# Query transfers on a second queue, idle transposes in the lead-in, a second PSUM bank up to slot 31, and a last tile stored in two halves

## Chip, core and metric

One core of one Trainium2 chip. The metric is device time in microseconds (us) of one execution; a kernel's time is the median of its executions. All runs told here gave the right result and were in the fast state. The program occupies one core. *Clock* means the share of its full clock that TensorE was granted, 1.00 or 0.50 in these traces; a mean below 1 tells how much of the time it was at half. A *window* at half clock is a stretch in which it was granted 0.50.

## The reference, cut to what matters

```python
# q, k, v: (8 batches, 8 heads, 576 rows, 64)   x = attention output as (4608, 512)
scores = scale * q @ k^T
scores = where(scores >= rowmax - tau, scores, -1e9)     # threshold mask
attn   = exp(scores - rowmax); attn /= attn.sum() + 1e-9
x      = (attn @ v) rearranged to (4608, 512)
h      = x @ w_in                                        # 512 -> 2048
g      = h * clip(h + 3, 0, 6) / 6
out    = g @ w_out                                       # 2048 -> 512
```

## The kernel before

Attention runs in 144 *slots*: 16 quads of heads (four heads of one batch) with nine slots each. A slot is 128 query rows of two heads. In each slot TensorE makes the scores, VectorE their row maximum, GpSimd the bias, ScalarE mask and exp, GpSimd the normalised weights, TensorE the value product. From slot 23 on the first product of the MLP of finished batches and its gate (`mm1`, from 80.69 us), from slot 31 on its second product too (`mm2`, from 111.61 us), are mixed into the slots; what is left of it runs after slot 143 without attention.

The parts that the change touches (cuts marked `...`):

```python
N1 = 22        # up to this slot VectorE copies keys out of PSUM, then ScalarE
N2 = 28        # up to this slot small products take two banks in turn
...
def main(dst, src, h, order):                     # one head of q or k, all on SyncE's queue
    nc.sync.dma_start(out=dst[:, :, h, :], in_=src[b, 4 * g + h, 0:512, :].rearrange(order, t=4))
...
def warm_up(count):                               # idle transposes: of a constant, the result isn't used
    warm = ps_h.tile([P, 2, 512], F32, tag="h", name="warm")
    for _ in range(count):
        nc.tensor.transpose(warm[:, 0, 0:P], identf[:], identf[:])
warm_up(14)
...
def bank(name):                                   # a bank of PSUM for a small product or transpose
    nonlocal turn
    turn += 1
    if now < N2 and turn % 2:
        return ps_o.tile([P, 512], F32, tag="o", name=name)
    return ps_m.tile([P, 512], F32, tag="m", name=name)

def copy_out(out, in_):                           # keys out of PSUM
    if 0 <= now < N1:
        nc.vector.tensor_copy(out=out, in_=in_)
    else:
        nc.scalar.copy(out=out, in_=in_)
...
evict = transpose_k(0); warm_up(4); evict_q = transpose_q(0)      # lead-in, shortened
evict(); evict_q()
transpose_rest(0)()          # remaining 64 rows of keys AND queries, one bank, VectorE then ScalarE
...
queue[0].tiles = scores(0, 0)
for n, sl in enumerate(queue):                    # the slots
    now = n
    ...                                           # exp of slot n-1, maxima of slot n
    if slot != 8 and todo1:
        h = mm1(item); r = mm1_relu(h, on_act=(slot in (0, 1, 3, 5))); mm1_gate(item, h, r)
    ...                                           # masks, transposes, value products
    if n + 1 < len(queue):
        queue[n + 1].tiles = scores(queue[n + 1].quad, queue[n + 1].slot)
    if n < 8:
        warm_up(6)
    ...
count = [0, 0]
def rest1(item, then):                            # MLP after the last slot
    h = mm1(item, pool=ps_s if count[0] % 3 else None)            # None: bank h
    count[0] += 1
    mm1_gate(item, h, mm1_relu(h, on_act=True))
```

The program gives each engine its own list of work in this order.

## Time and profile before

| quantity | value | where from |
|---|---|---|
| time, median of the first 3 runs | 561.12 us (561.0 to 562.59) | unprofiled runs |
| the execution that was profiled | 564.1 us, span 562.3 us, clock 0.989 | its own record |
| TensorE busy | 535.0 us, 95% | page |
| half clock in that execution | 10.9 to 17.8 and 106.5 to 109.9 us, and after the last product | clock records, windows of 0.5 us |

### The profile page before, as it was taken

To read this page: it belongs to the slowest core of one execution; us is meant where nothing else is said; L and a number is where in the kernel's file an instruction comes from. 1 tells how busy PE (TensorE), PEld (TensorE's weight loads), DVE (VectorE), ACT (ScalarE), POOL (GpSimd) and SP (SyncE) were. 2 spreads that over 40 slices of the span, in tenths; PEclk is the share of its full clock that TensorE was granted. 3 is DMA by queue.
4 is the path that set the end of the run, shared out by engine and by line. 5 is a ranking of instruction groups with operands and counts; after the bars stand their busy time and mean duration, and the time that the engine had idled before them with its cause. 6 is when DMAs were issued, how large, how long until landed. Compare 5 with 4: busy or idle time off the path is not lost.

```text
span 562.3 us, 11634 instructions
## 1 busy us (share of the span) xinstructions
PE 535.0 (95%) x3856; PEld 309.3 (55%) x3856; DVE 424.4 (75%) x1040; ACT 470.3 (84%) x999; POOL 305.2 (54%) x646
## 2 busy tenths in 40 slices
PE   7998798899999999999999999999999999999997
PEld 5665455455545565555555565655555565654663
DVE  3588787687878788787878798887978798883440
ACT  4799899798988999989898999899898999983540
POOL 1678878854556555655456555755556555561000
PEclk8899999899999999999999999999999999999999
DMA  5879999997689876978589867987699865453102
GB/s 110 135 110 166 162 160 184 207 148 144 112 159 153 151 153 127 208 139 155 114 150 170 159 137 146 174 160 146 127 137 175 167 124 117 101 109 86 38 20 75
DMA packets 286204, 77.52 MB, mean 138 GB/s; under 512 B 269248, under 2 KB 281536, under 8 KB 286144
## 3 DMA queue, kind: packets, MB, share of 16 engines
q1 hardware_dynamic: 268736, 67.86, 64.8%
q0 software_dynamic: 17408, 8.92, 13.7%
q8 instruction: 30, 0.49, 0.4%
q14 instruction: 30, 0.25, 0.2%
HBM read 36.70 MB, written 9.44 MB: 82 GB/s over the span
## 4 chain that ended last, share of the span: by engine, by line
PE 58%; DVE 11%; ACT 9%; issue 4%; POOL 1%; DMA 1%; SPq 1%; DVEq 0%; POOLq 0%
PE h L353 18%; PE o L382 17%; PE s L256 16%; DVE s L277 5%; ACT s L285 4%; PE av L323 3%; ACT s L290 3%; DVE g L370 2%; DVE r L364 2%; ACT r L362 2%; PE s L262 1%; PE tp L213 1%; PE ar L323 1%; DVE osb L390 1%; POOL pn L298 1%
## 5 line engine op out<-in xcount | busy, mean ns | idle before, releaser
L298 POOL TENSOR_SCALAR pn<-s,rinv 128x576 bf16<-128x576 f32 x288 | 211.6, 745 | 133.5 <-issue 58.5
L277 DVE TENSOR_SCALAR_CACHE_REDUCE s<-s 128x576 f32<-128x576 f32 x288 | 205.9, 752 | 44.9 <-PE s L256 35.2
L285 ACT ACTIVATE s<-s,bias 128x576 f32<-128x576 f32 x288 | 207.1, 766 | 36.8 <-POOL bias L280 35.7
L290 ACT ACTIVATE s<-s 128x576 f32<-128x576 f32 x288 | 192.7, 671 | 0.3
L256 PE MATMUL s<-kT,qT 64*128 64x288 f32 x1024 | 172.7, 435 | 5.4 <-DVE s L277 3.2
L353 PE MATMUL h<-xT,w_in_sb 128*128 128x320 bf16 (+1 forms) x1024 | 145.0, 287 | 5.5 <-DVE g L370 4.6
L382 PE MATMUL o<-w_out_sb,g 128*128 128x512 bf16 x576 | 140.9, 379 | 3.6 <-DVE osb L390 3.0
L353 PEld LDWEIGHTS <-w_in_sb 128*128 128x128 bf16 x1024 | 92.0, 97 | 68.4 <-issue 31.1
L256 PEld LDWEIGHTS s<-kT,qT 64*128 64x128 f32 x1024 | 94.8, 188 | 62.7 <-DVE s L277 24.9
L370 DVE SCALAR_TENSOR_TENSOR g<-r,h 128x512 bf16<-128x512 f32 (+1 forms) x128 | 96.4, 754 | 41.2 <-ACT r L362 39.3
L280 POOL TENSOR_SCALAR bias<-m 128x1 f32<-128x1 f32 x288 | 54.4, 189 | 69.0 <-DVE s L277 48.2
L382 PEld LDWEIGHTS <-g 128*128 128x128 bf16 x576 | 55.6, 98 | 58.2 <-issue 9.8
L362 ACT ACTIVATE r<-h,three 128x640 f32<-128x640 f32 (+1 forms) x74 | 54.4, 737 | 21.1 <-PE h L353 20.4
L290 ACT ACTIVATION_READ_ACCUMULATOR s<-s 128x1 f32 x288 | 54.2, 188 | 0.0
L364 DVE TENSOR_SCALAR r<-h 128x512 f32<-128x512 f32 (+1 forms) x54 | 40.5, 751 | 0.0
L390 DVE TENSOR_SCALAR osb<-o 128x512 f32<-128x512 f32 x31 | 21.0, 676 | 22.2 <-PE o L382 22.2
L323 PE MATMUL av<-pT,vm 128*64 128x512 bf16 x256 | 34.6, 392 | 2.0 <-ACT kT L203 2.0
L323 PEld LDWEIGHTS <-vm 128*64 128x64 bf16 x512 | 18.1, 111 | 25.2 <-issue 18.3
L293 DVE RECIPROCAL rinv<-rsum 128x2 f32<-128x2 f32 x144 | 23.0, 160 | 10.2 <-ACT s L290 9.5
L335 DVE CAST xT<-av 128x512 bf16<-128x512 f32 x32 | 21.8, 681 | 5.6 <-PE av L326 5.3
L277 DVE DVE_READ_ACCUMULATOR s<-s 128x1 f32 x288 | 23.9, 83 | 0.0
L388 ACT ACTIVATE osb<-o 128x512 f32<-128x512 f32 x5 | 3.0, 597 | 23.9 <-PE o L382 23.9
(42 smaller groups left out, 255.9 us busy)
## 6 DMA issues: line engine op xcount, KB each, us to landing
km<-in_k_dram SPq DMA_DIRECT2D x64, 128.0 KB, 3.0
out_dram<-osb SPq DMA_DIRECT2D x32, 256.0 KB, 2.4
nq<-in_q_dram SPq DMA_DIRECT2D x96, 72.0 KB, 2.7
vm<-in_v_dram POOLq DMA_DIRECT2D x16, 256.0 KB, 5.4
nq<-in_q_dram SPq DMA_DIRECT2D x16, 128.0 KB, 3.9
w_in_sb<-in_moe_w_in_dram POOLq DMA_DIRECT2D x16, 128.0 KB, 4.1
w_out_sb<-in_moe_w_out_dram POOLq DMA_DIRECT2D x16, 128.0 KB, 4.5
pT<-pn SPq DMA_TRANSPOSE x119, 3.4
```

The source lines that it names most:

```text
L256: nc.tensor.matmul(tiles[a][:, hf, 0:HALF], qT_of(pair)[a * 64:(a + 1) * 64, t * P:(t + 1) * P], keys(pair, a, hf), start=True, stop=True)
L277: nc.vector.tensor_scalar(out=sl.s[:, i, :].rearrange("p (a b) -> p a b", a=2), in0=ps[:, :, 0:HALF], scalar1=1.0, scalar2=None, op0=Alu.m ...
L280: nc.gpsimd.tensor_scalar(out=sl.bias[:, i:i + 1], in0=sl.m[:, i:i + 1], scalar1=-scale, scalar2=tau, op0=Alu.mult, op1=Alu.add)
L285: nc.scalar.activation(out=s, in_=s, func=Act.Prelu, bias=sl.bias[:, i:i + 1], scale=scale, alpha=REJECT)
L290: nc.scalar.activation(out=s, in_=s, func=Act.Exp, accum_out=sl.rsum[:, i:i + 1])
L298: nc.gpsimd.tensor_scalar(out=pn[:, i, :], in0=sl.s[:, i, :], scalar1=sl.rinv[:, i:i + 1], scalar2=1.0, op0=Alu.mult, op1=Alu.mult)
L323: nc.tensor.matmul(ps[a * 64:(a + 1) * 64, :], vm[:, 2 * hp + a, c * D:(c + 1) * D], pT[:, 5 * a + c, cols], start=(c == 0), stop=False)
L353: nc.tensor.matmul(hps[:, n, 0:w], w_in_sb[:, ki, (ni + n) * P:(ni + n + 1) * P], xT[b][:, ki, c0:c0 + w], start=(ki == 0), stop=(ki == KI ...
L362: nc.scalar.activation(out=r, in_=hps, func=Act.Relu, bias=three[:])
L364: nc.vector.tensor_scalar(out=r, in0=hps, scalar1=3.0, scalar2=0.0, op0=Alu.add, op1=Alu.max)
L370: nc.vector.scalar_tensor_tensor(out=gbuf[:, ni:ni + 2, c0:c0 + w], in0=r, scalar=6.0, in1=hps, op0=Alu.min, op1=Alu.mult)
L382: nc.tensor.matmul(o_ps[0], gbuf[:, ni, mt * P:(mt + 1) * P], w_out_sb[:, ni, :], start=(ni == 0), stop=(ni == NI - 1))
```

## The change

Four intents: the first scores shall not wait for query rows that are needed only in slot 8, and TensorE's clock shall stay up through the lead-in; the value product of slot 30 shall not wait for a PSUM bank; the first of the last output tiles shall find a free buffer; the last tile's eviction and store shall be split over two engines.

```diff
-    N2 = 28
+    N2 = 31
...
         def load_q(n):
...
+                    main(..., by=nc.scalar if quad == n == 0 else nc.sync)
...
-    def transpose_rest(quad):
+    def transpose_rest(quad, of_k=True, of_q=True):     # each half can be left out
...
-    transpose_rest(0)()
+    transpose_rest(0, of_q=False)()
+    warm_up(6)
...
+        elif n == 1:
+            evict = transpose_rest(0, of_k=False)
...
+        if n == 0:
+            warm_up(8)
         if n + 1 < len(queue):
             queue[n + 1].tiles = scores(...)
...
-    count = [0, 0]
+    count = [1, 0]
+    def last_out():
+        nc.scalar.activation(out=osb[:, 0:c], in_=o_ps[0][:, 0:c], func=Act.Copy, scale=1.0 / 6.0)
+        nc.scalar.dma_start(out=out[r0:r0 + P, 0:c], in_=osb[:, 0:c])
+        nc.vector.tensor_scalar_mul(out=osb[:, c:2 * c], in0=o_ps[0][:, c:2 * c], scalar1=1.0 / 6.0)
+        nc.sync.dma_start(out=out[r0:r0 + P, c:2 * c], in_=osb[:, c:2 * c])
...
-                late.extend(mm2_out(...))
+                if (bb, mt) == (B // 2 - 1, 8):
+                    last_out()
+                else:
+                    late.extend(mm2_out(...))
```

More of the change, by code (lines that the diff above doesn't have):

```diff
@@ L85, in load_quad, with main @@
         nq, km, kr = nat[quad]
-        def main(dst, src, h, order):
-            nc.sync.dma_start(out=dst[:, :, h, :], in_=src[b, 4 * g + h, 0:512, :].rearrange(order, t=4))
+        def main(dst, src, h, order, by=nc.sync):
+            by.dma_start(out=dst[:, :, h, :], in_=src[b, 4 * g + h, 0:512, :].rearrange(order, t=4))
         def blocks_q(n, a, j):
@@ L97, in load_q @@
                 for a in range(2):
-                    main(nq[:, 0:1024].rearrange("p (t h d) -> p t h d", h=4, t=4), q, 2 * n + a, "(t p) d -> p t d")
+                    main(nq[:, 0:1024].rearrange("p (t h d) -> p t h d", h=4, t=4), q, 2 * n + a, "(t p) d -> p t d",
+                         by=nc.scalar if quad == n == 0 else nc.sync)
             else:
@@ L226, in transpose_k @@
         return lambda: copy_out(kT_of(pair)[:, 64:576], ps[:])
-    def transpose_rest(quad):
+    def transpose_rest(quad, of_k=True, of_q=True):
         ps = bank("tr")
         nq, _, kr = nat[quad]
-        nc.tensor.transpose(ps[:, 0:P], kr[:], identf[:])
-        if by_pe(2 * quad):
+        of_q = of_q and by_pe(2 * quad)
+        if of_k:
+            nc.tensor.transpose(ps[:, 0:P], kr[:], identf[:])
+        if of_q:
             nc.tensor.transpose(ps[:, P:2 * P], nq[:, 1024:1152], identf[:])
@@ L237, in evict @@
             both = ps[:].rearrange("p (w n t) -> p w n t", n=2, t=64)
-            if by_pe(2 * quad):
+            if of_q:
                 nc.vector.tensor_copy(out=qT[:, :, 512:S], in_=both[:, 1])
-            copy_out(kT[0:64, :, S:S + 64], both[0:64, 0])
-            copy_out(kT[64:P, :, 0:64], both[64:P, 0])
+            if of_k:
+                copy_out(kT[0:64, :, S:S + 64], both[0:64, 0])
+                copy_out(kT[64:P, :, 0:64], both[64:P, 0])
         return evict
@@ L525 @@
     last = NQUAD - 1
-    count = [0, 0]
+    count = [1, 0]
+    def last_out():
+        osb = o_pool.tile([P, d_model], F32, tag="osb", name="osb")
+        r0, c = B * S - 64 - P, d_model // 2
+        nc.scalar.activation(out=osb[:, 0:c], in_=o_ps[0][:, 0:c], func=Act.Copy, scale=1.0 / 6.0)
+        nc.scalar.dma_start(out=out[r0:r0 + P, 0:c], in_=osb[:, 0:c])
+        nc.vector.tensor_scalar_mul(out=osb[:, c:2 * c], in0=o_ps[0][:, c:2 * c], scalar1=1.0 / 6.0)
+        nc.sync.dma_start(out=out[r0:r0 + P, c:2 * c], in_=osb[:, c:2 * c])
     def rest1(item, then):
@@ L539, in rest2 @@
                 flush()
-                late.extend(mm2_out(bb, mt, on_act=(count[1] % 2 == 0)))
+                if (bb, mt) == (B // 2 - 1, 8):
+                    last_out()
+                else:
+                    late.extend(mm2_out(bb, mt, on_act=(count[1] % 2 == 0)))
                 count[1] += 1
```

## The prediction

> **What bounds the kernel now.** I read the page first, then the stretches of time in which the granted clock fell, then the timeline of the first 20 us and of the change from attention alone to attention plus MLP (around 105 us), and last the chain of waits at the end.
>
> ```profile
> PE 535.0 (95%) x3856; PEld 309.3 (55%) x3856; DVE 424.4 (75%) x1040; ACT 470.3 (84%) x999; POOL 305.2 (54%) x646
> PE   7998798899999999999999999999999999999997
> ...
> L323 PE MATMUL av<-pT,vm 128*64 128x512 bf16 x256 | 34.6, 392 | 2.0 <-ACT kT L203 2.0
> ```
>
> TensorE is the bound for most of the span: from 113 to 504 us it is busy for 384.93 of 391 us. The parts with gaps are the head, the stretch to 113 us and a few waits at the end; the change works only on these. The last line shows one wait of TensorE for a ScalarE copy of keys, 2.0 us in the whole run.
>
> The windows of 1 us (columns: TensorE, weight loads, VectorE, ScalarE, GpSimd busy, granted clock, DMA):
>
> ```profile
> 9.00:10.00 1.00, 1.00 (x6) 0.51 (x6) 0.36 (x1) 0.00 (x0) 0.00 (x0) 1.00 1.03 232
> 11.00:12.00 1.00, 1.00 (x5) 0.72 (x5) 0.08 (x2) 1.00 (x2) 0.77 (x2) 0.50 0.44 97
> 16.00:17.00 1.00, 1.00 (x6) 0.28 (x2) 0.00 (x0) 0.64 (x2) 0.80 (x2) 0.50 0.00 0
> 18.00:19.00 1.00, 1.00 (x11) 0.81 (x10) 0.95 (x4) 0.78 (x2) 0.41 (x3) 1.00 0.86 106
> ```
>
> From 11 to 17.6 us TensorE runs at half its clock. The timeline of the same stretch:
>
> ```profile
> 7.59 0.30 PE L233 MATMUL tr<-identf,nq 128*128 128x128 f32 x1 [0.81 <-DMA nq<-in_q_dram]
> 8.25 0.53 ACT L203 COPY kT<-tr 64x128 f32<-64x128 f32 x2 [2.16 <-DVE qT L239]
> 8.83 1.23 PE L256 MATMUL s<-kT,qT 64*128 64x288 f32 x6 [0.27 <-ACT kT L203]
> 9.64 0.76 DVE L277 TENSOR_SCALAR_CACHE_REDUCE s<-s 128x576 f32<-128x576 f32 x1 [1.42 <-PE s L256]
> 10.46 2.96 PE L256 MATMUL s<-kT,qT 64*128 64x288 f32 x8 [0.39 <-DVE s L277]
> 17.14 0.76 DVE L277 TENSOR_SCALAR_CACHE_REDUCE s<-s 128x576 f32<-128x576 f32 x1 [2.84 <-PE s L256]
> 18.23 1.45 ACT L285 ACTIVATE s<-s,bias 128x576 f32<-128x576 f32 x2 [1.59 <-POOL bias L280]
> 106.35 0.56 ACT L203 COPY kT<-tp 128x512 f32<-128x512 f32 x1
> 106.96 1.92 PE L323 MATMUL av<-pT,vm 128*64 128x512 bf16 x8 [2.03 <-ACT kT L203]
> ```
>
> The first scores wait for the remainder of the queries (the last 64 rows), which no score needs before slot 8: transfer, transpose, VectorE copy, then the ScalarE copy of the remainder of the keys, which the first scores do need. Then the scores of slot 1 take 2.96 us where eight such matmuls take 1.24 us at full clock (at 18.61 us), so VectorE and ScalarE stand idle before slot 2. The end, from the chain of waits:
>
> ```profile
> 540.07 0.70 DVE g L370
> 540.77 0.04 issue
> 540.81 17.44 PE o L382 x80
> 558.25 0.02 issue
> 558.27 0.60 ACT osb L388
> ```
>
> The last five output tiles start only when a gate has emptied a PSUM buffer (TensorE idle 0.62 us), then 80 matmuls without a gap, one eviction of 0.60 us and the last store.
>
> [...] the first 14, alone on TensorE, take 3.06 us (0.21 us apart), and after them six take 0.88 us (0.12 apart)[...]. So I count on idle transposes. [...] The trace shows issues of 0.5 to 0.7 us each, one behind another, on SyncE. [...] the ScalarE copy at 8.25 us waited for the VectorE copy out of the same bank.
>
> **The change part by part.**
>
> Queries on ScalarE's queue, remainder of the queries later. TensorE's lead-in from the first key transpose (4.83 us) to the end of the transpose of the remaining keys (6.47 + 0.30 = 6.77) has almost no gap, so earlier queries by themselves gain nothing; what gains is that the 0.81 us wait and the transpose after it leave the path. The new path: ScalarE copies the keys' remainder from about 6.8 to 7.35 us while six idle transposes run to about 7.45; the scores of slot 0 begin there, and VectorE's maximum follows 1.36 us later (as at 119.89 to 121.25), at 8.8 instead of 9.64. Gain 0.8 us.
>
> Idle transposes (six before the first scores, eight behind them). Eight at 0.12 us fill about 8.6 to 9.65, just until VectorE has emptied the first score tile (8.8 + 0.76), so they delay nothing, and if the clock holds, slot 1's scores take 1.24 us from 9.65 and their maximum starts at 11.0 (now 12.51). Slot by slot on ScalarE: mask of slot 0 at 10.72 - 0.83 = 9.9; a slot's mask and exp take about 2.8 (10.72 to 13.50), so mask 1 at 12.7, mask 2 at 15.4 if its scores are there: scores 2 from about 11.9, maximum 13.25, bias ready 14.3, yes. Now mask 2 is at 18.23. Gain in all 2.8 to 2.9 us, the 0.8 included. From slot 3 on the same instructions follow in the same distances, and ScalarE is nearly full to 78 us (61.28 of 74 us, waits under 0.6 us each), so the gain is carried on.
>
> Two banks up to slot 31 (two names in turn until 28 before). In slot 30 the value product needs the single bank that the key transposes of slot 29 hold until the ScalarE copy at 106.35 ends; TensorE then stands 2.03 us and the clock falls (0.50 at 107 to 109 us), so the product takes 2.3 us instead of 1.43. With the second bank it runs from 104.9 to 106.35. But the next scores need that same copy of keys (106.9), and the next MLP product needs the gate which ends at 109.55, behind ScalarE's work and GpSimd's bias (108.58, GpSimd full with DMA issues and normalising from 97.5 us). So that product starts at 109.55 instead of 110.72, and the following scores at 112.0 instead of 113.0. Of 2.0 us about 1.0 remains.
>
> Counter of the last products started at 1. The buffers come in turn h, s, s. Now the last two items take both s buffers, and the first output tile wants the older (gate ended at 540.77). With the turn moved by one, the last item takes h, and the output tile wants the buffer of the third last, whose gate ended at about 539.89, before the last product ends at 540.2. Gain 0.6 us. The wait of 0.66 us at 508.56 stays: three buffers are in turn either way.
>
> Last tile in halves. From 128x640 against 128x512 (0.79 and 0.69 on ScalarE, 0.82 and 0.69 on VectorE) an element costs 0.8 and 1.0 ns, so halves take 0.40 and 0.43. They would save 0.2 us side by side, but [...]in the built program VectorE's half waits for ScalarE's count. One after another: 0.83 plus 0.05 for the hand-over, 0.28 later than now; the second store has half the bytes[...]. Net 0.
>
> Sum: 2.85 + 1.0 + 0.6 + 0 = 4.45 us; 561.12 - 4.45 = 556.7.
>
> **Rivals.** First, the clock falls in spite of the idle transposes[...]: then slot 1 still suffers, about 1.5 to 2 us of the head's gain are lost, 558.5. For it: TensorE was 70 to 80% busy in 7.6 to 11.0 and it fell. Against: from 18 to 30 us a like density with the same fillers kept it at 1.00. I give it 20%. Second, [...]the keys land later: the engines moved 126 and 150 GB/s at 2 to 4 us and 254 at 4 to 5, so there is room, but the 512 KB might still land at 5.2 instead of 4.8; 557.1. Third, the head's gain is eaten before 78 us by transfers (the DMA part is busy there); no instruction waits there for a transfer of inputs or weights, so I give it 10%; 559.5. Fourth, the second bank brings the whole 2 to 3 us, if GpSimd and ScalarE follow faster than I worked out; 555.
>
> **Range and chances.** Runs of the kernel before spread from 561.0 to 562.6. Weighing the rivals I predict 556.8, eight in ten between 555.2 and 558.8. Faster by over 2% needs 549.9, more than all idle time I found on the path; slower by over 2% has no mechanism here.
>
> **What would show it.** Right: the first maximum of VectorE at 8.7 to 9.0 us, granted clock 1.00 from 9 to 18 us, mask 2 near 15.4; no wait of the value product for the key copy, clock 1.00 at 107; the first of the 80 last matmuls without a wait; VectorE's last half after ScalarE's. Wrong: a half-clock window before 20 us, first key transposes after 5.2 us, or the same distance of 3 us no longer present at 78 us.

The sum is as recorded: 2.85 + 1.0 + 0.6 + 0 = 4.45 us, 556.7 us; none of its four terms is cut. Of the 0 for the halves one part is: against the eviction that ends 0.28 us later stood an earlier landing of the second store, whose size was my guess. That idle transposes would keep the clock up, on which 2.0 of the 2.85 us rest, was my estimate, drawn from the spacing of the first transposes (0.21, then 0.12 us); no trace had shown it.

## The result and the profile after

The changed kernel took 560.57 us (559.83 to 562.68, six runs) against 562.65 us (561.0 to 563.4, six runs, the first three among them) for the kernel before in the same rounds. The ratio is 0.9974, 95% interval 0.995 to 0.9998. Ratios here and below are the mean time of one kernel's runs over that of the other's of the same rounds, so they are not quite the ratio of the medians quoted. All outputs are right. The class is "same", as predicted; the time lies outside the predicted range (555.2 to 558.8), 3.8 us above the predicted 556.8.

The page of the changed kernel, engines' busy time and the value product's group:

```profile
PE 531.9 (95%) x3829; PEld 309.5 (55%) x3870; DVE 424.8 (76%) x1041; ACT 469.9 (84%) x999; POOL 305.3 (55%) x646
...
L327 PE MATMUL av<-pT,vm 128*64 128x512 bf16 x256 | 34.6, 393 | 0.0
```

The wait of the value product for a key copy (2.0 us before) is gone. The head, from the timeline of the changed kernel (start us, duration, engine and line, instruction, idle time before it and what ended it):

```profile
5.03 0.64 PE L214 MATMUL tp<-identf,km 128*128 128x128 f32 x4 [0.41 <-DMA km<-in_k_dram]
...
6.70 0.53 ACT L204 COPY kT<-tr 64x128 f32<-64x128 f32 x2 [0.42 <-PE tr L234]
7.32 1.24 PE L260 MATMUL s<-kT,qT 64*128 64x288 f32 x8
8.59 0.76 DVE L281 TENSOR_SCALAR_CACHE_REDUCE s<-s 128x576 f32<-128x576 f32 x1 [1.33 <-PE s L260]
...
10.89 0.76 DVE L281 TENSOR_SCALAR_CACHE_REDUCE s<-s 128x576 f32<-128x576 f32 x1 [0.86 <-PE s L260]
...
15.26 1.44 ACT L289 ACTIVATE s<-s,bias 128x576 f32<-128x576 f32 x2
```

First maximum at 8.59 (predicted 8.8), that of slot 1 at 10.89 (predicted 11.0), mask of slot 2 at 15.26 (predicted 15.4, before 18.23). Views of 1 us each (TensorE, weight loads, VectorE, ScalarE, GpSimd busy, granted clock, DMA):

```profile
9.00:10.00 1.00, 1.00 (x8) 0.65 (x6) 1.00 (x4) 0.32 (x1) 0.19 (x1) 1.00 0.98 207
11.00:12.00 1.00, 1.00 (x9) 0.75 (x7) 1.00 (x3) 1.00 (x4) 0.49 (x2) 1.00 0.00 0
16.00:17.00 1.00, 0.98 (x8) 0.70 (x7) 0.93 (x3) 1.00 (x3) 1.00 (x2) 1.00 0.69 62
60.00:61.00 1.00, 1.00 (x7) 0.61 (x9) 0.08 (x1) 0.89 (x4) 1.00 (x2) 0.50 1.24 204
108.00:109.00 1.00, 1.00 (x7) 0.67 (x6) 1.00 (x4) 1.00 (x4) 1.00 (x2) 0.50 0.71 139
```

The third number from the end is the clock: full in the head, as hoped, but half at 60 us, where it was full before, and still half at 108 us.

The region of slots 30 and 31, same kernel, timeline:

```profile
102.81 1.05 PE L327 MATMUL av<-pT,vm 128*64 128x512 bf16 x8
...
104.30 0.56 ACT L204 COPY kT<-tp 128x512 f32<-128x512 f32 x1
...
104.91 1.24 PE L260 MATMUL s<-kT,qT 64*128 64x288 f32 x8 [0.83 <-ACT kT L204]
...
106.81 0.69 DVE L374 SCALAR_TENSOR_TENSOR g<-r,h 128x512 bf16<-128x512 f32 x1 [3.42 <-ACT r L366]
...
107.55 1.86 PE L357 MATMUL h<-xT,w_in_sb 128*128 128x256 bf16 x8 [1.40 <-DVE g L374]
```

The value product runs at once; TensorE's gap has moved to two later places, 0.83 us before the next scores (which need the same key copy) and 1.40 us before the next MLP product (which needs the gate). That product then takes 1.86 us, at half clock. The end:

```profile
538.26 17.43 PE L386 MATMUL o<-w_out_sb,g 128*128 128x512 bf16 x78
...
555.72 0.38 ACT L541 ACTIVATE osb<-o 128x256 f32<-128x256 f32 x1 [6.31 <-PE o L386]
556.14 0.37 ACTq L542 DMA_DIRECT2D out_dram<-osb  x1
556.14 0.42 DVE L543 TENSOR_SCALAR osb<-o 128x256 f32<-128x256 f32 x1 [3.12 <-ACT osb L541]
556.59 0.33 SPq L544 DMA_DIRECT2D out_dram<-osb  x1
```

The last output products start without the 0.62 us wait for a gate; the two halves run one after the other.

To place a gain in time I compare, slot by slot, the start of the slot's first VectorE maximum in two traces. I call *lead* the number of microseconds by which a slot starts earlier than in the first profile of the kernel before. For the changed kernel:

| slot (time before, us) | lead, changed kernel |
|---|---|
| 0 (9.64) | 1.05 |
| 4 (24.21) | 3.32 |
| 17 (61.87) | 3.32 |
| 18 (66.22) | 2.04 |
| 28 (97.17) | 2.05 |
| 31 (110.92) | 2.85 |
| 35 | 1.76 |
| 143 (502.51) | 1.76 |
| end of span | 2.5 |

So in the traces 3.3 us were won in the head, 1.3 lost at 60 us, 0.3 lost net around 107 us, and 0.7 won at the end. The trace thus shows 2.5 of the predicted 4.45 us; the losses lie where the clock was at half. The theory to be tested: the head's gain in the traces is not one of the change; the kernel before has half clock at 11 to 17.6 us only in some executions, and the profiled one happened to be such. The rival: the kernel before always has it, and the gain of the head is real but lost later to windows that the change itself provokes (60 us).

### The profile page after: what moved, and what is told of

Read it like the earlier page. It is cut to its first block, busy times and chain, and to the rows that moved or that the text cites. A ratio compares the mean times of both kernels' runs of the same rounds, so it can differ in the third digit from the quotient of the medians.

```text
span 559.8 us, 11625 instructions
## 1 busy us (share of the span) xinstructions
PE 531.9 (95%) x3829; PEld 309.5 (55%) x3870; DVE 424.8 (76%) x1041; ACT 469.9 (84%) x999; POOL 305.3 (55%) x646
## 4 chain that ended last, share of the span: by engine, by line
PE 62%; DVE 11%; ACT 7%; issue 3%; POOL 1%; SPq 1%; DMA 1%; DVEq 0%; POOLq 0%
PE h L357 19%; PE o L386 18%; PE s L260 17%; DVE s L281 4%; PE av L327 4%; ACT s L289 3%; ACT s L294 2%; DVE g L374 2%; DVE r L368 2%; ACT r L366 1%; PE s L266 1%; PE tp L214 1%; DMA nq<-in_q_dram 1%; PE ar L327 1%; DVE osb L394 1%
## 5 line engine op out<-in xcount | busy, mean ns | idle before, releaser
L260 PE MATMUL s<-kT,qT 64*128 64x288 f32 x1024 | 169.8, 430 | 6.0 <-DVE s L281 2.8
L386 PE MATMUL o<-w_out_sb,g 128*128 128x512 bf16 x535 | 134.1, 380 | 5.3 <-DVE osb L394 3.0
L266 PE MATMUL s<-kT,qT 64*64 64x288 f32 x256 | 20.1, 415 | 0.7 <-DVE s L281 0.7
```

The lines of the kernel that those rows point to most:

```text
L260: nc.tensor.matmul(tiles[a][:, hf, 0:HALF], qT_of(pair)[a * 64:(a + 1) * 64, t * P:(t + 1) * P], keys(pair, a, hf), start=True, stop=True)
L386: nc.tensor.matmul(o_ps[0], gbuf[:, ni, mt * P:(mt + 1) * P], w_out_sb[:, ni, :], start=(ni == 0), stop=(ni == NI - 1))
```

## The experiments

Line numbers differ by a few between the kernels.

### The kernel before, unchanged, profiled again

No edit.

> The kernel before, unchanged, to see its own spread and the clock of each run. Theory A (the half-clock windows of TensorE fall in different places from run to run[...]): the runs spread over 2 us or more, the mean granted clock of the runs differs (0.985 to 0.998), the runs with the higher clock are the shorter ones, and this profile has its half-clock windows in other places than the one before (there 11 to 17.6 us and 106 to 110 us). Theory B (the windows are fixed by the program): all runs have about the clock 0.989 and the profile shows the same two windows.

562.94 us (562.04 to 564.39), ratio 1.002 (1.0002 to 1.0038): the comparison of a kernel with itself leaves about 0.2%, a measure of what the ratios can resolve. Its profiled execution (562.04 us, clock 0.995) has no half clock in the head. Views of 1 us, then the timeline:

```profile
10.00:11.00 1.00, 0.61 (x3) 0.29 (x2) 1.00 (x3) 0.17 (x1) 0.19 (x1) 1.00 0.84 191
11.00:12.00 1.00, 1.00 (x7) 0.66 (x6) 0.19 (x2) 1.00 (x2) 0.67 (x2) 1.00 0.41 93
16.00:17.00 1.00, 1.00 (x9) 0.70 (x8) 0.70 (x2) 0.86 (x3) 0.74 (x4) 1.00 0.12 7
```

```profile
4.79 0.99 PE L213 MATMUL tp<-identf,km 128*128 128x128 f32 x4 [0.17 <-DMA km<-in_k_dram]
...
9.74 0.76 DVE L277 TENSOR_SCALAR_CACHE_REDUCE s<-s 128x576 f32<-128x576 f32 x1 [1.42 <-PE s L256]
...
10.56 1.91 PE L256 MATMUL s<-kT,qT 64*128 64x288 f32 x8 [0.39 <-DVE s L277]
...
16.41 1.44 ACT L285 ACTIVATE s<-s,bias 128x576 f32<-128x576 f32 x2
```

The same program, with the same gaps and none of the added idle transposes (*fillers* below), runs slot 1's scores in 1.91 us instead of 2.96 and has mask 2 at 16.41 instead of 18.23. Its lead at slot 4 is 2.16 us and stays so (2.17 at slot 28). Of the 3.3 us of the first comparison, 2.2 are thus the difference between two executions of the kernel before. Before the last product half clock fell here only at 104.5 to 107.9 us.

### The changed kernel, unchanged, profiled again

No edit.

> The changed kernel, unchanged. Theory A: the lag of its slots behind those of the kernel before is again 3.3 us up to slot 17 or differs there only where the other profile has a window; the loss of 1.27 us at slot 18 is gone or elsewhere, and the total loss goes with the half-clock time in the profile. Theory B (something in the program, a transfer or GpSimd, costs 1.3 us at slot 18 each time): the loss at slot 18 is there again with the clock at 1.00. Time about 560.5 in either case.

560.02 us (559.34 to 560.38), ratio 0.9961 (0.9947 to 0.9976). Leads: 3.15 at slot 4, 3.15 at slots 18 and 28, 3.95 at slot 35. There is no half clock at 60 us; there is a window at 93.9 to 97.3 us, of which no loss is left at slot 35. The two executions of the changed kernel around 59 to 63 us, TensorE's timeline; first the original profile, then this one:

```profile
59.26 1.44 PE L318 MATMUL pt<-identb,pn 128*128 128x128 bf16 x9 [0.90 <-POOL pn L302]
60.63 1.92 PE L327 MATMUL av<-pT,vm 128*64 128x512 bf16 x8
62.34 0.57 PE L330 MATMUL av<-pT,vr 128*64 128x512 bf16 x2
```

```profile
59.42 0.40 PE L318 MATMUL pt<-identb,pn 128*128 128x128 bf16 x4 [0.90 <-POOL pn L302]
60.14 0.45 PE L318 MATMUL pt<-identb,pn 128*128 128x128 bf16 x5 [0.33 <-POOL pn L302]
60.53 1.05 PE L327 MATMUL av<-pT,vm 128*64 128x512 bf16 x8
61.41 0.38 PE L330 MATMUL av<-pT,vr 128*64 128x512 bf16 x2
```

Both have the same gap of 0.90 us for GpSimd's weights ahead of the transposes; in one the clock fell after it and eight products took 1.92 us, in the other 1.05. So the loss at 60 us isn't a fixed consequence of the change, which speaks against the rival.

The clock records kept in the traces say more. In each of the 14 profiles of this document the first record is a rise to full clock, between 4.10 and 7.10 us, and all 38 later changes lie a whole number of equal steps after it, to within 0.01 us. The step is measured: in the first profile of the kernel before the last change lies 556.37 us after the first rise, 163 steps of 3.4133 us. I call *marks* the times that lie whole steps after an execution's first rise; at most of them the clock stayed as it was. I move each profile's marks by its lead at slot 17, to have them all in the program's time: at the marks at 62.46, 62.58 and 62.61 us the clock fell (the falls near 60 us of three traces), and at those at 62.33 or earlier, or at 62.96 or later, it didn't fall there (thirteen profiles; the kernel with fillers in many slots is left out). Among the kernels with the new head the fall at this place thus went with where the marks lay; why isn't shown. No profile with the old head has a mark in that range, so that it would lose there too isn't shown, though its instructions there are the same.

Profile against profile without windows in the head or at 60 us (this one against the second one of the kernel before), the spans are 557.6 and 560.2: 2.6 us, of which 0.99 is in place at slot 4, 0.89 more at slot 35, and 0.71 at the end.

### The head alone

The changed kernel with the other parts undone:

```diff
-    N2 = 31
+    N2 = 28
-    count = [1, 0]
+    count = [0, 0]
-                if (bb, mt) == (B // 2 - 1, 8):
+                if False:
```

> Only the head's part of the change (queries on the second queue, remainder of the queries in slot 1, idle transposes); two banks up to slot 28, counter 0, last tile whole. My step of the prediction: 2.85 us faster than before, and 1.6 slower than the whole change. Theory A: 1 to 2.5 us faster than before in the median, because the kernel before does not have its half-clock window in the head in every run; at most 1 us slower than the whole change.

561.87 us (560.16 to 562.18), ratio 0.9991 (0.9975 to 1.0007): about 0.5 us, not distinguishable from nothing, and below the 1 to 2.5 us expected. The trace shows one way in which the head's gain can vanish altogether:

```profile
5.23 1.09 PE L214 MATMUL tp<-identf,km 128*128 128x128 f32 x4 [0.61 <-DMA km<-in_k_dram]
...
9.66 0.76 DVE L281 TENSOR_SCALAR_CACHE_REDUCE s<-s 128x576 f32<-128x576 f32 x1 [1.33 <-PE s L260]
```

The clock had not risen yet when the key transposes began (the trace's first clock record is a rise at 7.05 us): they took 1.09 us here, against 0.64 in the profile of the changed kernel; the first maximum came at 9.66, no sooner than before. In the kernel before the same event costs little: in its second profile (rise at 5.54 us) the key transposes took 0.99 us, and the maximum came at 9.74 against 9.64, because TensorE waits for the last query rows until 7.6 us anyway. By taking that wait away the change has laid the clock at the start bare.

### All but the head

The changed kernel with the head as before:

```diff
-                         by=nc.scalar if quad == n == 0 else nc.sync)
+                         by=nc.sync)
-    transpose_rest(0, of_q=False)()
-    warm_up(6)
+    transpose_rest(0)()
-        elif n == 1:
-            evict = transpose_rest(0, of_k=False)
-        if n == 0:
-            warm_up(8)
```

> Only the other parts (two banks up to slot 31, counter from 1, last tile in halves); the head as before. My steps of the prediction: 1.6 us faster than before (1.0 + 0.6 + 0). Reading of the trace of the changed kernel: 0.5 us faster (the second bank gives -0.3, the counter +0.6 to 0.8, the halves 0), and TensorE's gap is found before the next MLP product instead of before the value product.

560.3 us (559.89 to 561.76), ratio 0.9973 (0.9957 to 0.9989): about 1.5 us, where 0.5 was expected from the first trace of the changed kernel. The lead grows by 0.81 us from slot 28 (2.11) to slot 35 (2.92), and from slot 143 to the last eviction by a further 0.8. To the end of the span it grows by 1.3; some 0.4 of this lies after the landing of the last store, in the program's closing. In this execution no window fell on slot 31, and the same two products as in the changed kernel's profile took:

```profile
107.49 1.03 PE L357 MATMUL h<-xT,w_in_sb 128*128 128x256 bf16 x8 [1.39 <-DVE g L374]
...
108.36 1.03 PE L386 MATMUL o<-w_out_sb,g 128*128 128x512 bf16 x4
```

The wait of 1.39 us for the gate is there, with or without the window; the window adds its own loss. Head alone (0.5) and all but the head (1.5) add up to 2.0 us, against 2.2 for the whole change in the same rounds (0.39% of 562.2): no interaction is needed.

### Are the idle transposes what holds the clock in the head?

First the kernel before with the change's idle transposes at the same two places and nothing else; then the changed kernel without them.

```diff
 # the kernel before, with fillers
     transpose_rest(0)()
+    warm_up(6)
...
+        if n == 0:
+            warm_up(8)
```

> The kernel before with nothing but the idle transposes of the change (six ahead of the first scores, eight behind them). My prediction's step: they take away the half-clock window of the head, 2.0 us of the 2.85. Theory A (the kernel before has that window in a few of its runs only): the median is 0 to 0.6 us shorter, and what goes are the longest runs (563.5 and more); in the profile slots 4 to 28 stand 2.0 to 2.3 us earlier than in the first profile of before and within 0.3 us of the second one.

562.04 us (561.35 to 565.71), ratio 1.0005 (0.998 to 1.003). One of its runs took 565.71 us at clock 0.990, so fillers did not rule out the slowest executions either.

```diff
 # the changed kernel, without fillers
-    warm_up(6)
...
-        if n == 0:
-            warm_up(8)
```

> The changed kernel without its added idle transposes. My prediction's step: 2.0 us slower than the whole change. Theory A: 0 to 0.7 us slower in the median, one run or more with a half-clock window in the head 2 us slower; without such a window slot 4 is as early as in the whole change.

559.96 us (559.51 to 560.6), ratio 0.9959 (0.9942 to 0.9976), the same as with them (0.9961). Its lead at slot 4 is 3.09 us against 3.15. Within what these rounds resolve, some 0.2%, the idle transposes are worth nothing in either kernel. I can't exclude that they avert a rare window.

### Filling TensorE's gaps elsewhere

Two of the falls lie at a wait of TensorE: that at 106.50 us in the first profile of the kernel before (wait of 2.03 us, to 106.96) and that at 59.30 us in the changed kernel's (0.90 us, to 59.26). If the waits bring the falls about, which no trace shows, idle transposes could keep them off. First eleven in slot 30, which lies in the 1.4 us gap before the gate; then also four in each of the slots 8 to 21 and 26 to 29.

```diff
+        if n == 30:
+            fill(11, ps_m)          # 11 idle transposes into the free bank
```

> The changed kernel with 11 more idle transposes (about 1.3 us) in slot 30, into the bank that stands empty, where TensorE waits 1.4 us for a gate ahead of the MLP product of slot 31. Theory A: no half-clock window at 104 to 111 us in the profile, slots from 33 on are 0.8 to 1.1 us earlier against slot 30 in every run, so 0.3 to 0.6 us faster than the change in the median (its profiles had that window in one of two). If instead the window does not matter, the time is that of the change, 560.0.

559.82 us (559.61 to 560.96), ratio 0.9959 (0.9942 to 0.9976): no different from the changed kernel. In its profile slot 31 ran at full clock and the lead grew by 0.81 us from slot 28 to 35, as it did in other executions without these fillers.

```diff
+        elif n < 22:
+            warm_up(4)
+        if n in (26, 27, 28, 29):
+            fill(4, ps_o if n in (26, 27, 29) else ps_m)
```

> As the last, and four idle transposes (0.5 us) also in slots 8 to 21 and 26 to 29. Theory A: granted clock 1.000 up to the last output in every run, all runs within 0.5 us of each other but for the start, 0.5 to 1 us faster than the change: 559.2. Against it: the fillers stand ahead of products that TensorE could have started, each up to 0.5 us, which shows as slots of more than 3.0 us before slot 22 and makes it slower than the change.

561.62 us (560.42 to 564.18), ratio 0.9991 (0.9965 to 1.0016). Its profile has no half-clock window before the last matmul (mean 0.999), yet the gain is mostly gone: the lead falls from 3.17 at slot 4 to 2.21 at slot 28, and by another 1.34 us from slot 31 to 32, where TensorE waits for a transposing transfer (waits of TensorE: for what, total us, count, longest):

```profile
PE ar L333 <- DMA pR<-pn: 1.6, 1, 1.6
```

Five of its six runs list a clock of 0.999 or more, of the changed kernel's twelve three do. So such fillers seem to hold the clock, but they stand in TensorE's list ahead of real work: in this profile, without any window, 0.96 us is lost between slots 4 and 28, about as much as a window takes. That the late transfer follows from the fillers isn't shown; it appeared in this run alone.

### Two improvements on the changed kernel

The first splits the first keys over both queues, one head each, so that neither queue issues two key transfers before the queries.

```diff
-            loads.append(lambda n=n: [main(km, k, ...) for a in range(2)])
+            loads.append(lambda n=n: [main(km, k, ..., by=nc.scalar if quad == n == 0 and a else nc.sync)
+                                      for a in range(2)])
-                         by=nc.scalar if quad == n == 0 else nc.sync)
+                         by=nc.scalar if quad == n == 0 and a else nc.sync)
```

> The changed kernel with the first keys on both queues too: one head's keys and queries from SyncE, the other's from ScalarE. In the changed kernel's profiles the first key transposes start at 5.03 and 5.19 us, in the kernel before at 4.83 and 4.79: issuing keys beside queries made the keys later. [...]the transposes start at 4.4 to 4.7 us and slots 4 to 28 are 0.3 to 0.6 us earlier (lag 3.4 to 3.8 us against the first profile of before); 559.6 in the median. If the landing time is fixed by the bytes of all four transfers together, they start at 5.0 to 5.2 again and nothing changes.

559.58 us (559.45 to 563.95), ratio 0.9972 (0.9947 to 0.9998). The key transposes start at 4.41 us instead of 5.03 to 5.25, but in the profiled execution they ran at the low clock, and the first maximum came at 8.68, no sooner than 8.59:

```profile
4.41 1.06 PE L215 MATMUL tp<-identf,km 128*128 128x128 f32 x4
```

The second moves the key copy of slot 29 from ScalarE to VectorE, which takes it out of the list of ScalarE work ahead of the gate.

```diff
-        if 0 <= now < N1:
+        if 0 <= now < N1 or now == 29:
```

> The changed kernel with the copy of the keys in slot 29 on VectorE in place of ScalarE. My reading is that the second bank gave 0.8 us and not 2 because ScalarE, in order, makes this copy (0.56) ahead of the exp and the relu of slot 30, on which the gate and the MLP product of slot 31 wait, while VectorE stands idle 3.42 us ahead of that gate. Then the gate is 0.5 us earlier and slots from 31 on gain 0.4 to 0.6 us (lag against slot 28 of 1.2 to 1.4 in place of 0.8). Rival: GpSimd's bias is the limit, and nothing changes.

559.37 us (558.57 to 560.59), ratio 0.9953 (0.9937 to 0.997). Its timeline around slot 31:

```profile
101.89 0.67 DVE L202 COPY kT<-tp 128x512 f32<-128x512 f32 x1
...
106.30 0.69 DVE L374 SCALAR_TENSOR_TENSOR g<-r,h 128x512 bf16<-128x512 f32 x1 [2.38 <-ACT r L366]
...
107.04 1.03 PE L357 MATMUL h<-xT,w_in_sb 128*128 128x256 bf16 x8 [1.82 <-DVE g L374]
```

The copy ends at 102.6 and the gate starts at 106.30 instead of 106.81. The lead grows by 1.29 us from slot 28 (2.08) to slot 35 (3.37), against 0.80 without this edit: the ScalarE copy was part of what kept the second bank from its full worth. The head of this execution was one with the low clock (key transposes 1.09 us, lead at slot 4 only 2.20), and yet its median lies 0.9 us below the changed kernel's 560.31. The two were not timed in the same rounds, and the intervals of their ratios (0.9953 here, 0.9961 for the changed kernel) overlap: that it is faster is shown by the trace's slots 28 to 35, not by the times.

Both together (the two diffs above, nothing else):

> Both of these on the changed kernel: the sum of the two, 559.2 us in the median, if each holds; the head's part shows up to slot 28 and the copy's from slot 31.

558.86 us (557.9 to 559.32), ratio 0.9942 (0.9928 to 0.9957), 3.1 us below the median of the kernel before in the same rounds, 561.92. Here the early keys met the full clock:

```profile
4.29 0.61 PE L215 MATMUL tp<-identf,km 128*128 128x128 f32 x4
...
6.82 1.24 PE L261 MATMUL s<-kT,qT 64*128 64x288 f32 x8
```

The lead is 3.82 at slot 4, falls to 2.55 at slot 18 through a window at 58.5 to 62.5 us, and is 3.85 at slot 35. This version beats the kernel before beyond doubt; it lies 1.4 us below the median of the changed kernel (560.31, twelve runs of two sessions), with which it was not timed in the same rounds.

### The last tile whole

```diff
-                if (bb, mt) == (B // 2 - 1, 8):
+                if False:
```

> The changed kernel with its last tile evicted and stored whole, as before, by ScalarE (the counter stays at 1). My step: the halves are worth 0, since VectorE's half waits for ScalarE's. From the maximum of slot 143 to the end of the span the changed kernel takes 59.05 us and the kernel before 59.75 to 59.8; if the counter alone gives that difference, this one takes 59.0 to 59.2, and the median is that of the change, about 560.1. If the halves give a part, it takes 59.3 or more.

560.62 us (559.4 to 560.92), ratio 0.996 (0.9933 to 0.9986), against 0.9961 with halves. Its end, from the timeline:

```profile
537.33 17.43 PE L386 MATMUL o<-w_out_sb,g 128*128 128x512 bf16 x78
...
554.80 0.60 ACT L392 ACTIVATE osb<-o 128x512 f32<-128x512 f32 x1 [6.31 <-PE o L386]
```

From the first maximum of slot 143 to the start of the last tile's eviction it took 54.98 us, the two profiles of the changed kernel 54.97 and 54.98, those of the kernel before 55.76 and 55.76: the moved counter is worth 0.78 us. The last store landed 57.61 us after that maximum, in the changed kernel 57.56, in the kernel before 58.39: the halves are worth 0.05 us. The ends of the spans say less (59.18, 59.05 and 59.04, 59.79 and 59.75 us after the maximum), because the closing of the program after that landing took 0.99 to 1.52 us in the 14 profiles.

## Why the prediction was wrong

The waits went and came where the prediction said. What failed is the size of the head's term, of which the larger part was a half clock that the idle transposes were to cure, and the number from which the sum was taken.

**The step that failed: "Now mask 2 is at 18.23. Gain in all 2.8 to 2.9 us."** The changed kernel did what the step says: mask 2 at 15.26. But 18.23 belongs to the one execution that was profiled, not to the kernel: in the second profile of the kernel before it is at 16.41, and slot 4 starts 2.16 us earlier. The prediction took the half clock from 11.0 to 17.6 us for a lasting property that the idle transposes would cure. Fillers in the kernel before (1.0005; the interval allows a gain of 0.2%, 1.1 us, at most) and the changed kernel without fillers (0.9959, with them 0.9961) show no gain from them that the rounds resolve. The listed clocks agree: 6.83 us at half clock alone takes the mean to 0.994, and 32 of the 50 later executions of the kernel before list 0.995 or more, so at least these had no such stretch to cure. I even named, as a rival, that the clock may fall in spite of the idle transposes, but only as a danger to the changed kernel; whether it falls in every execution should have been asked of the kernel before as well. A reading is off, too: "1.24 us at full clock" is the time of scores that wait for nothing (1.27 at 18.61 us). Slot 1's second half waits for VectorE to empty a bank, so at full clock slot 1's scores took 1.91 us in the kernel before and 1.81 in the changed one; of the 2.96 us only 1.05 was the clock. Their first maximum came at 10.89 as predicted nevertheless.

**What stands in its place.** Against a head of the kernel before without that window, the lead at slot 4 is 1.15, 0.99, 0.93, 0.69, 1.01 and 1.02 us in six profiles with the new head (the changed kernel's two, that without fillers, the two with more of them, the whole last tile), about what the reorder was to give (0.8), and 0.08 and 0.04 where the clock rose only at 7.05 and 7.10 us, after the key transposes (the head alone, and the key copy on VectorE; the old head with a rise at 7.04, in the run of all but the head, stands at -0.05). Timed, the head is worth some 0.5 us, which isn't distinguishable from nothing.

**The number subtracted from.** 561.12 us was a median of three. The 50 executions of the kernel before have a median of 562.24 us (560.96 to 565.59), and they follow the clock that each run lists: the 18 at 0.997 or more have a median of 561.41, the 14 at 0.995 or 0.996 of 562.30, the 18 below of 563.48. The profile came from an execution of 564.1 us at 0.989. So I took losses that only a slow execution has off a time that faster executions had. The baseline was 1.1 us too low, which would have brought the estimate nearer to what came (562.24 - 4.45 = 557.8), and the overstated head outweighed it.

**Second bank, predicted 1.0.** Nearly right where no window falls on slot 31: 0.8 us (five profiles), but -0.3 and -0.5 in the two where one did, the first of the changed kernel and that of the whole last tile. All four profiles with the single bank have such a window, which begins within 1.4 us of the end of the 2.0 us wait; of the ten with the second bank these two have. So the 0.8 us compares executions without the window to ones with it, and where both have it nothing was gained: keeping the clock up may be most of what the second bank is worth, which no run tested by itself. The prediction saw that the gate would be the next wait; what it left out is that a half-clock window can fall there after as well as before. Putting the key copy on VectorE brought the step to 1.3.

**Counter, predicted 0.6.** Right in kind, 0.78 us in size, and the first of the last products no longer waits. **Halves, predicted 0.** Right: they run one after the other, and bring 0.05 us.

**The keys, second rival.** Partly true: key transposes began at 5.03 to 5.25 us in the eight profiles of the changed head against 4.56 to 4.88 in the four of the old one. Split over both queues they began at 4.41 and 4.29; one issue of keys had taken 0.7 us (two 1.36, first profile of the kernel before).

**"The gain is carried on" to 78 us.** True in five profiles with the new head (leads at slots 4 and 28 equal within 0.1 us); in the first profiled run of the changed kernel, that without fillers and that with both improvements a window at 58.5 to 63 us took 1.2 to 1.3 us of it. The loss of 1.0 us with fillers in slots 8 to 29 fell in a profile without any window there, so I put it down to the fillers. No trace shows the third rival, transfers, before 78 us.

The account in the traces, in us:

| stretch | first profiles, before and changed | second profiles |
|---|---|---|
| head, to slot 4 | 3.32 | 0.99 |
| slot 4 to 28 | -1.27 | -0.01 |
| slot 28 to 35 | -0.29 | 0.90 |
| slot 143 to the end | 0.74 | 0.71 |
| sum of spans' difference | 2.5 | 2.6 |

That the sums agree is luck: in the first pair the head holds 2.3 us more than in the second, nearly all of it the half clock of the kernel before (2.16), and the windows at 60 and 107 us took about as much from the changed kernel (1.3 and 1.2 us less than in the second pair). Timed, the change is worth 1.9 us on the medians of the 50 later runs of the kernel before and of twelve runs of the changed one (562.24 against 560.31, of several chips), 0.3 to 0.4% by the ratios.

**What stays open.** How often the kernel before has its 6.8 us of half clock in the head: in at most 18 of the 50 runs, but a run's mean clock tells how many windows there were, not where, and it leaves out the low clock before the first rise. Why the clock is low at some key transposes is read from the traces: in eight of the 14 profiles the first rise came after they had begun (rise at 5.30 to 7.10 us), in six before (4.10 to 5.18). The column of the granted clock doesn't show it: it says 1.00 from the start, because the clock records begin with the first rise; before it the durations tell (in the first profile of the kernel before, f32 transposes lie 0.21 us apart before the rise at 4.10 us, 0.11 after it; four key transposes take 0.63 us, or 1.09 where the rise came late). In all 14 profiles TensorE ran only f32 transposes up to the rise.

What places the marks in an execution is open; no run controlled it. What makes the clock fall at one is open, too, and how busy TensorE was doesn't tell by itself. By the profile's busy time the 3.41 us before a fall had 79% (7.51 to 10.93 us, kernel before) and 56% (the 3.41 us before 59.29 us, changed kernel: 1.91 us busy, no gap longer than 0.90); with 47% (103.13 to 106.54 us, both improvements) no fall followed. The stretch of 18 to 30 us, which the prediction calls of like density to the 7.6 to 11.0 us before the fall, had 90% against 81%, and stayed at 1.00. So a kernel whose TensorE is 95% busy had half clock in its middle, in other places in each execution: from 11, 59, 94, 105 or 107 us.

## What to carry to other kernels

Before a gap or a slow stretch in a profile is counted as a gain, look at whether the profiled execution is a typical one: compare its own time and clock with the other runs, and profile the unchanged kernel a second time if a lost clock carries the argument. Compare slots with slots only after looking where each trace's clock records lie. Losses that come and go with the run belong to both kernels' averages and must not be taken off one. When a buffer wait is removed, follow the in-order lists of the engines behind it: the next wait, here a gate held up by a ScalarE copy, showed a further half microsecond that a one-line move to VectorE gained in two traces.
